# Two narrow first-stage units two turns later, and one copy of two chains on ScalarE

## The chip, the cores and the metric

The kernel runs on one core of a Trainium2 chip. The metric is the device time of one execution in microseconds (us). The engines are PE (TensorE, matmuls; PEld is its weight load), DVE (VectorE), ACT (ScalarE), POOL (GpSimd) and SP (SyncE, which here only issues DMA transfers). Each engine runs its own queue in order and waits on semaphores for the others.

## The reference

The input `x` is 8 batches of 2496 tokens with 256 channels. It is filtered in the frequency domain, and a soft mixture of experts with 8 experts of 4 slots follows over all 19968 tokens:

```
X = rfft(x, axis=1);  y = irfft(X * (filt_r + 1j*filt_i))
t = y.reshape(19968, 256)
logits = t @ phi                          # 32 slots
d = softmax over tokens (axis 0) of logits
slot_out[e] = relu((d.T @ t)[e] @ w1[e]) @ w2[e]
out = (softmax over slots (axis 1) of logits) @ slot_out
```

## The kernel before

The transform of 2496 = 39 x 64 points is done in two stages of matmuls. **First stage** (batches 1 to 7): each batch is cut into 6 pieces, `PIECE`, the piece 0 half as wide as the others. A piece is loaded to SBUF as `xt` (`load_x`, six buffers), folded into sums and differences `eo` (`fold_x`, L329, two elementwise instructions, on POOL but for the first pieces; two buffers), multiplied on PE (`s1_unit`, L346, matmuls at L357) into a PSUM tile of the pool `ps_s1`, which has one buffer (L264), copied by ACT to SBUF as `at` (L366, four buffers), and stored to `a_dram` in memory (`store_a`, L371). A piece of a batch is called unit (batch, piece) below. Batch 0 has a first stage of its own ahead of the loop.

**Main loop.** It runs over 80 turns n, ten a batch (`CPB = 10`), and writes out each turn's work in this order: loads of `ash` (the first stage's result, back from `a_dram`; `load_to`, L818), the load of one more `xt` and the fold of the units of turn n+1 (`split_next`, L788), the stores of the unit of the turn before, `t_unit` of turn n-2 (transposes, L467, ACT copies the result to `y`), `x_unit` of turn n (second-stage matmuls, L435; then DVE multiplies with the filter, `t2` at L455 and L457, and combines to `yt` at L458 and L459), the first-stage units of turn n, in odd turns `l_unit` (the logits, L494), and two steps of the chains (`hop_slot`, L861). At which turn a unit stands says `slot_of` (L78): the `ash` loads of a batch follow three turns behind its piece 5. In turns 33 to 37 stand (4,4), (5,0), (4,5), none, (5,1).

**Chains.** For each group of batches, (0,1), (2,3), (4,5), (6), (7), a generator `chain(g)` (L530) turns logits into running softmax weights and sums up the weighted tokens. Its steps run between the turns: transposes of the logits (`ltr`), inverse transforms (`v1`, `v`, `lg`), the maximum, the exponentials of `d` (DVE subtracts at L634, ACT exponentiates at L635, three pieces), their transform `u` (matmuls L528, ACT copies at L663), transposes of `u` (L525) copied to `u2` (L674), the transform `dd` (ACT copies at L682), the sums `z` and `s`. The first three chains take turns between two PSUM banks (`ps_c`, L263). In chains 0 to 2 the copy to `u2` goes in three parts, t0 = 0, 4 and 8, of 4, 4 and 2 transposes.

After the loop come the experts (weights loaded while the last turns run) and the output stage, whose stores end the execution.

Within the order of the program, the instructions of each engine are put in line when the kernel is built, by a planner that simulates them; `not_before` and `behind` add orders by hand, and the matmuls of `s1_unit` have high priority.

Of the kernel before, what the change touches and what calls it, by code (L numbers as in the profile page):

```python
# [39 lines left out]
NG = len(GROUPS)  # L40
# [8 lines left out]
CPB = NT // 2  # L49
# [4 lines left out]
NU = len(PIECE)  # L54
# [23 lines left out]
def slot_of(b, u):  # L78

    if b == 1:  # L80
        return u - 1
    if (b, u) in ((2, NU - 1), (3, 0)):
        return 2 * CPB - 6 + b - 2
    return CPB * b - 5 - (2 * (NU - 1 - u) if u else CPB + (b > 2))


def freq_of(t, c):
# [167 lines left out]
def fft_soft_moe(ctx, tc, x0, w0, x, ff, phi, wx, cst, w1q, sgn, out):  # L255
    nc = tc.nc
    pe, dve, act, pool_e, sp = nc.tensor, nc.vector, nc.scalar, nc.gpsimd, nc.sync
# [266 lines left out]
    def pe_t(*a):  # L524
        line(pe.transpose(*a))  # L525
# [4 lines left out]
    def chain(g):  # L530
# [6 lines left out]
        def psum(shape, name):  # L537
            pool, tag = banks[turn[0] % len(banks)]
            turn[0] += 1
            return pool.tile(shape, F32, tag=tag, name=name)  # L540
# [20 lines left out]
        for t0 in range(0, NT, 7):  # L561
# [3 lines left out]
            n = min(7, NT - t0)  # L565
# [19 lines left out]
        for s0 in range(0, NH, SA):  # L585
            n = min(SA, NH - s0)
# [6 lines left out]
        for s0 in range(0, NH, SA):  # L593
            n = min(SA, NH - s0)
# [33 lines left out]
        u = wk.tile([P, HT, 2 * N2], F32, tag="ca", name=f"u_{g}", bufs=1)  # L628
# [13 lines left out]
        for a0 in range(0, NH, 4):  # L642
            n = min(4, NH - a0)
            if a0 + 4 < NH and not late:
                dispatch(a0 + 4)
            pu = psum([P, 2, 4 * PK * 2, HT], f"u_{g}_{a0}")
# [19 lines left out]
        ended = [None, None]  # L666
        u2 = wk.tile([P, HT, 2, nb, SLOTS], F32, tag="cc", name=f"u2_{g}", bufs=1)
        dd = wk.tile([P, HT, 2, nb, SLOTS], F32, tag="cb", name=f"dd_{g}", bufs=1)
        for t0 in range(0, HT, TG):
            n = min(TG, HT - t0)  # L670
            pu = psum([P, TG, R], f"u2_{g}_{t0}")
            for t in range(n):
                pe_t(pu[:, t, :], u[0:R, t0 + t, :], ident[0:R, 0:R])
            ended[1] = dve.tensor_copy(u2[:, t0 : t0 + n].rearrange("k t h b e -> k t (h b e)"), pu[:, 0:n])  # L674
            yield f"u2_{t0}"
        for t0 in range(0, HT, TG):
            n = min(TG, HT - t0)
# [30 lines left out]
        for k, (ti, th, b2) in enumerate(terms):  # L708
            j = k % 4
            t = th * HT + ti  # L710
# [68 lines left out]
    for b, u in units[1:]:  # L779
        at_slot.setdefault(slot_of(b, u), []).append((b, u))  # L780
# [37 lines left out]
    def load_to(n):  # L818
        while loads:
            b, c = loads[0]  # L820
            if n < max(b * CPB + c - (3 if b < 2 else ASH), slot_of(b, NU - 1) + (2 if b < 3 else 3)):
                break
            load_ash(*loads.pop(0))
# [74 lines left out]
    for n in range(NS + LT):  # L898
        if n < NS:
            if n == slot_of(2, NU - 1) + 1:  # L900
                store_a()
            load_to(n)
            if n == CPB // 2:
                issue(cst_t[:, NEAR:FAR], cst[:, NEAR:FAR])
            if n == NS - 2 * CPB:
                behind("sp", sp.dma_start(cst_t[:, FAR:], cst[:, FAR:]))
            split_next(n + 1)
            store_a()
# [23 lines left out]
        if n >= LT:  # L932
            b, c = divmod(n - LT, CPB)
            if c % 2 == 1:
                l_unit(b, c)
            if c == CPB - 1 and b in last and b < BATCH - 1:
                active.append((last[b], chain(last[b])))
            if (b, c) == (BATCH - 1, CPB - 2):
                final = chain(NG - 1)
                for _ in range(3):  # L940
                    next(final)
# [11 lines left out]
    k = NS % YB - CPB  # L953
# [201 lines left out]
```

## Time and profile before

| | us |
|---|---|
| median of 3 runs (375.1 to 376.7) | 375.63 |
| profiled execution | 375.31 |
| its span, first to last instruction | 373.5 |
| PE busy in it | 344.2 |
| DVE, ACT, POOL busy in it | 264.6, 175.2, 147.0 |

The profiled execution takes 1.8 us more than its span. PE is the busiest engine; its granted clock is at the upper of its two levels (2.4 GHz) up to some 340 us, where the outputs are being stored, and at the lower one (1.2 GHz) behind that. How to read it: PE's time without work inside the loop is what one looks for, and what ends it. A wait for several semaphores is put down to the one that came last by the profile, so the engine named is not always the one that held things up.

### The profile page before, as it was taken

What the parts mean: (1) busy time and instruction counts of PE and PEld (TensorE: products, weight loads), DVE (VectorE), ACT (ScalarE), POOL (GpSimd) and SP (SyncE); (2) the same over time, 40 slices, a digit from 0 to 9 for tenths busy, and PEclk for the clock granted to TensorE, in tenths of its full rate; (3) what the DMA queues carried; (4) which work ended last, traced back from release to release, by engine and by line L of the source; (5) the groups of instructions that cost most, each with busy time, mean ns of one, the idle gap of its engine ahead of it and who ended that gap; (6) DMA issues with size and microseconds to landing.
All of it is one profiled execution on the core that took longest, in us unless ns stands there. A gap on an engine that the chain in (4) does not pass through costs nothing. (4 is left out here: it accounts for less than half of the span.)

```text
span 373.5 us, 10516 instructions
## 1 busy us (share of the span) xinstructions
PE 344.2 (92%) x4254; PEld 255.9 (69%) x4254; DVE 264.6 (71%) x522; ACT 175.2 (47%) x354; POOL 147.0 (39%) x177
## 2 busy tenths in 40 slices
PE   8999999899998899999889998899989999999950
PEld 6866766677776577867666775777866635878850
DVE  1586897778998969689996847695675552887540
ACT  3466554454555444545625453533354430766430
POOL 0188655545546213724830754332631302650000
PEclk9999999999999999999999999999999999999555
DMA  8999899799799459979853747642898993699996
GB/s 300 395 396 371 291 329 355 233 342 374 222 350 335 143 163 301 314 235 292 307 185 80 224 138 215 255 142 58 299 355 280 326 272 83 253 411 413 417 419 287
DMA packets 50438, 104.17 MB, mean 279 GB/s; under 512 B 5250, under 2 KB 23810, under 8 KB 48214
## 3 DMA queue, kind: packets, MB, share of 16 engines
q1 hardware_dynamic: 49700, 103.16, 79.4%
q8 instruction: 33, 0.54, 0.6%
q10 hardware_dynamic: 690, 0.35, 0.3%
q14 instruction: 15, 0.12, 0.1%
HBM read 63.37 MB, written 40.12 MB: 277 GB/s over the span
## 5 line engine op out<-in xcount | busy, mean ns | idle before, releaser
L435 PE MATMUL x<-cst_t,ash 128*128 128x128 f32 x640 | 85.7, 276 | 1.7 <-DMA ash<-a_dram 1.7
L455 DVE TENSOR_TENSOR t<-x,ff_t 128x512 f32<-128x512 f32 x80 | 55.1, 689 | 39.0 <-PE x L435 30.5
L336 POOL TENSOR_TENSOR eo<-xt 128x512 f32<-128x512 f32 (+1 forms) x37 | 45.2, 1220 | 94.4 <-issue 89.8
L435 PEld LDWEIGHTS x<-cst_t,ash 128*128 128x128 f32 x640 | 78.1, 192 | 4.0 <-DMA ash<-a_dram 2.6
L366 ACT COPY at<-s 128x1024 f32<-128x1024 f32 (+1 forms) x42 | 39.6, 942 | 47.8 <-PE s L357 27.8
L467 PE MATMUL t<-cst_t,yt 128*128 128x128 f32 x320 | 49.9, 278 | 0.0
L339 POOL TENSOR_TENSOR eo<-xt 128x512 f32<-128x512 f32 (+1 forms) x40 | 48.9, 1221 | 0.0
L481 ACT COPY y<-t 128x512 f32<-128x512 f32 x58 | 33.8, 587 | 30.8 <-PE t L467 30.5
L357 PE MATMUL s<-eo,w1q_t 64*64 64x512 f32 (+1 forms) x336 | 42.8, 579 | 2.7 <-POOL eo L339 2.5
L467 PEld LDWEIGHTS t<-cst_t,yt 128*128 128x128 f32 x320 | 35.9, 141 | 10.2 <-issue 7.1
L457 DVE TENSOR_TENSOR x<-x,ff_t 128x512 f32<-128x512 f32 x60 | 41.7, 696 | 1.3
L1104 PE MATMUL out<-so,st 32*128 32x256 f32 x468 | 35.1, 337 | 2.4 <-ACT ob L1109 1.3
L1104 PEld LDWEIGHTS out<-so,st 32*128 32x128 f32 x468 | 30.7, 222 | 6.1 <-ACT ob L1109 2.9
L494 PEld LDWEIGHTS l<-yt,phi_t 128*32 128x32 f32 x640 | 15.2, 109 | 25.5 <-issue 21.1
L1109 DVE COPY ob<-out 128x512 f32<-128x512 f32 (+1 forms) x40 | 25.0, 669 | 8.5 <-DMA out<-ob 5.8
L458 POOL TENSOR_TENSOR yt<-yt,t 128x256 f32<-128x256 f32 x20 | 15.1, 754 | 35.0 <-DVE yt L457 25.4
L1109 ACT COPY ob<-out 128x512 f32<-128x512 f32 (+1 forms) x40 | 21.7, 582 | 14.8 <-DMA out<-ob 7.8
L458 DVE TENSOR_TENSOR yt<-x,t 128x256 f32<-128x256 f32 x60 | 25.2, 420 | 1.3
L494 PE MATMUL l<-yt,phi_t 128*32 128x128 f32 x640 | 25.7, 278 | 0.0
L459 DVE TENSOR_TENSOR yt<-x,t 128x256 f32<-128x256 f32 x60 | 24.8, 413 | 0.0
L528 PE MATMUL s<-y,dd 128*32 128x256 f32 x232 | 19.2, 381 | 0.3 <-ACT dd L682 0.3
L528 PE MATMUL u<-cst_t,d 117*64 117x60 f32 (+3 forms) x440 | 15.2, 221 | 1.2 <-ACT d L635 1.2
(117 smaller groups left out, 482.1 us busy)
## 6 DMA issues: line engine op xcount, KB each, us to landing
xt<-in_x SPq DMA_DIRECT2D x35, 512.0 KB
ash<-a_dram SPq DMA_DIRECT2D x70, 256.0 KB
out<-ob SPq DMA_DIRECT2D x17, 1024.0 KB
a_dram<-at SPq DMA_DIRECT2D x56, 240.0 KB
w<-in_wx SPq DMA_DIRECT2D x33, 256.0 KB
w<-in_wx SPq DMA_DIRECT2D x6, 512.0 KB
x_t<-in_x SPq DMA_DIRECT2D x5, 512.0 KB
ff_t<-in_ff SPq DMA_DIRECT2D x10, 256.0 KB
```

Of the source, the lines that this page charges most:

```text
L336: ins = (dve if (1, 2) < (b, u) < (2, 0) else eng).tensor_tensor(out=eo[:, 0, 0:n], in0=xs[:, :, 0], in1=xs[:, :, 1], op=ALU.add)
L339: ins = eng.tensor_tensor(out=eo[:, 1, 0:n], in0=xs[:, :, 0], in1=xs[:, :, 1], op=ALU.subtract)
L357: ins = pe.matmul(ps, w1q_t[q, c], eo[q, c, 0:n], start=True, stop=True)
L366: act.copy(at[:, 0:n], both[:, :, 0:n].rearrange("q r u d -> q u r d"))
L435: ins = pe.matmul(ps[:, 2 * k + dh].rearrange("q r c -> q (r c)"), ash[:, k, dh * P : (dh + 1) * P], C("a1" if t0 + k else "b0"), start=Tr ...
L455: dve.tensor_tensor(out=t2, in0=ps[:, :, ::-1, :], in1=fiv, op=ALU.mult)
L457: dve.tensor_tensor(out=part, in0=ps, in1=frv, op=ALU.mult)
L458: add.tensor_tensor(out=yt[:, :, 1, :], in0=part[:, :, 1, :], in1=t2[:, :, 1, :], op=ALU.add)
L467: ins = pe.transpose(pt[:, k, dh, :], yt[:, c % 2, 2 * k + dh].rearrange("q r c -> q (r c)"), ident)
L494: ins = pe.matmul(pl[32 * j : 32 * j + 32, :], phi_t[:, dh, :], yt[:, j // 2, 2 * (j % 2) + dh].rearrange("q r c -> q (r c)"), start=(dh = ...
L1104: nc.tensor.matmul(prs[k][:, mm, :], sts[n][q, hs, c0 : c0 + P], so[q, ho], start=(i == 0), stop=(i == 2))
L1109: copy(ob[:, nm * k : nm * (k + 1), :], prs[k])
```

## The change

Two edits. In `slot_of`, the narrow unit of piece 0 stands at turn 10b - 16 for batches over 2 (one turn ahead of piece 5 of the batch before); for batches 5 and 7 it now stands at 10b - 14. So (5,0) goes from turn 34 to 36 and (7,0) from 54 to 56, and the order is (4,5), (5,0), (5,1) where it was (5,0), (4,5), (5,1). Its fold, its load's place in SP's queue and its stores go with it. In `chain`, the first of the three copies to `u2` (t0 = 0) is an ACT copy in the chains 0 and 1 (g < NG - 3 = 2) where it was a DVE copy.

```diff
--- before.py
+++ after.py
@@ -81,7 +81,7 @@
         return u - 1
     if (b, u) in ((2, NU - 1), (3, 0)):
         return 2 * CPB - 6 + b - 2
-    return CPB * b - 5 - (2 * (NU - 1 - u) if u else CPB + (b > 2))
+    return CPB * b - 5 - (2 * (NU - 1 - u) if u else CPB + (1, -1)[b in (5, 7)] * (b > 2))
 
 
 def freq_of(t, c):
@@ -671,7 +671,8 @@
             pu = psum([P, TG, R], f"u2_{g}_{t0}")
             for t in range(n):
                 pe_t(pu[:, t, :], u[0:R, t0 + t, :], ident[0:R, 0:R])
-            ended[1] = dve.tensor_copy(u2[:, t0 : t0 + n].rearrange("k t h b e -> k t (h b e)"), pu[:, 0:n])
+            copy = act.copy if t0 == 0 and g < NG - 3 else dve.tensor_copy
+            ended[1] = copy(u2[:, t0 : t0 + n].rearrange("k t h b e -> k t (h b e)"), pu[:, 0:n])
             yield f"u2_{t0}"
         for t0 in range(0, HT, TG):
             n = min(TG, HT - t0)
```

## Rows read from the trace of the kernel before

**Rows 1.** The page's first part: busy us, share, instructions of each engine.

```profile
PE 344.2 (92%) x4254; PEld 255.9 (69%) x4254; DVE 264.6 (71%) x522; ACT 175.2 (47%) x354; POOL 147.0 (39%) x177
```

**Rows 2.** Busy us of each engine (instructions) by stretches; then clock, DMA.

```profile
70.00:80.00 10.00, 10.00 (x110) 7.16 (x108) 9.47 (x20) 4.71 (x9) 3.94 (x4) 1.00 0.93 287
110.00:120.00 10.00, 8.75 (x136) 6.91 (x133) 8.63 (x15) 6.41 (x14) 8.03 (x6) 1.00 0.99 357
```

**Rows 3.** Waits of PE: engine, line, releaser: us in total, times, longest.

```profile
PE s L357 <- POOL eo L339: 2.5, 2, 1.2
PE u L525 <- DVE u L674: 1.7, 2, 0.9
PE x L435 <- DMA ash<-a_dram: 1.7, 4, 1.1
```

**Rows 4.** PE in order of time: start, us, line, out<-in, count, [idle before].

```profile
87.12 1.09 PE L357 MATMUL s<-eo,w1q_t 64*64 64x512 f32 x8
...
111.80 0.66 PE L357 MATMUL s<-eo,w1q_t 64*64 64x256 f32 x8
...
116.03 1.09 PE L357 MATMUL s<-eo,w1q_t 64*64 64x512 f32 x8 [1.25 <-POOL eo L339]
...
118.94 0.66 PE L467 MATMUL t<-cst_t,yt 128*128 128x128 f32 x4
```

**Rows 5.** The same of POOL: the folds of the first stage's inputs.

```profile
86.26 1.27 POOL L339 TENSOR_TENSOR eo<-xt 128x512 f32<-128x512 f32 x1
...
105.19 0.73 POOL L336 TENSOR_TENSOR eo<-xt 128x256 f32<-128x256 f32 x1 [2.58 <-issue]
...
110.88 1.28 POOL L339 TENSOR_TENSOR eo<-xt 128x512 f32<-128x512 f32 x1
112.63 1.82 POOL L336 TENSOR_TENSOR eo<-xt 128x512 f32<-128x512 f32 x1 [0.47 <-POOL eo L339]
114.40 1.59 POOL L339 TENSOR_TENSOR eo<-xt 128x512 f32<-128x512 f32 x1
```

**Rows 6.** The same of ACT, around the first wait.

```profile
114.89 0.52 ACT L635 ACTIVATE d<-d 117x384 f32<-117x384 f32 x1 [0.93 <-DVE d L634]
115.32 0.57 ACT L366 COPY at<-s 128x512 f32<-128x512 f32 x1
```

**Rows 7.** DVE's L634 from 111 us (ns min/median/max); then DVE in order.

```profile
L634 DVE TENSOR_TENSOR d<-lg,m_run x3: 679/1254/1631, 111.4 to 113.2; 117x512 f32<-117x512 f32 x2, 117x384 f32<-117x384 f32 x1
...
113.23 1.63 DVE L634 TENSOR_TENSOR d<-lg,m_run 117x384 f32<-117x384 f32 x1
...
117.03 0.41 DVE L459 TENSOR_TENSOR yt<-x,t 128x256 f32<-128x256 f32 x1
```

**Rows 8.** Order of time at the second place, DVE and PE.

```profile
182.65 1.25 DVE L694 TENSOR_TENSOR al<-m_run,m_run 128x32 f32<-128x32 f32 x1
...
183.90 1.09 PE L357 MATMUL s<-eo,w1q_t 64*64 64x512 f32 x8 [1.24 <-POOL eo L339]
...
186.17 0.41 DVE L459 TENSOR_TENSOR yt<-x,t 128x256 f32<-128x256 f32 x1
...
186.80 0.66 PE L467 MATMUL t<-cst_t,yt 128*128 128x128 f32 x4
```

**Rows 9.** The `u2` step of chain 0 in order; last, ACT copies grouped.

```profile
124.05 1.01 ACT L366 COPY at<-s 128x1024 f32<-128x1024 f32 x1 [2.07 <-issue]
...
125.09 1.28 DVE L674 COPY u<-u 128x512 f32<-128x512 f32 x2
...
125.83 0.44 PE L525 MATMUL u<-cst_t,u 128*128 128x128 f32 x2 [0.86 <-DVE u L674]
126.42 2.72 PE L528 MATMUL dd<-u,cst_t 128*128 128x512 f32 x8 [0.16 <-DVE u L674]
...
L481 ACT COPY y<-t 128x512 f32<-128x512 f32 x58 | 33.8, 587 | 30.8 <-PE t L467 30.5
```

**Rows 10.** Waits of SP's queue behind 255 us (columns as in rows 3).

```profile
SPq L882 <- PE ltr L525: 5.9, 1, 5.9
```

## The prediction

> **What bounds the kernel now.** I read the engines' totals first, then busy time by stretches of 10 us, then the waits of PE, and then the order of events around the longest of them. PE is busy 344.2 of 373.5 us [rows 1]; in an ordinary stretch of the main loop it is busy 10.00 of 10.00, and it falls to 8.75 in that from 110 to 120 us [rows 2]; the same pattern comes back 68 us later. So the loop is bound by PE, and what can be won there is PE's idle time. The waits of PE name two things that the change touches: two waits of a first-stage matmul (L357), 1.2 us each, and two of chain transposes (L525) on a DVE copy of `u2`, 0.9 us each [rows 3]. In these stretches PE has no other work that could fill them, since it runs its queue in order; each us of them should reach the end.
>
> **The first wait, and what ends it.** The narrow matmul at 111.80 is unit (5,0) (batch 5, piece 0, turn 34); the wide one at 116.03, with 1.25 us of idle PE before it, is (4,5) of turn 35 [rows 4]. The trace names the fold L339 that ends at 114.40 + 1.59 = 115.99 as the releaser. Counting folds against units, that is not this unit's fold: the narrow fold at 105.19 is that of (5,0), the next wide one, ending at 110.88 + 1.28 = 112.16, is that of (4,5), and the one from 112.63 is (5,1)'s, which could only start when (5,0) had freed one of the two `eo` buffers [rows 5]. Ten turns earlier the unit after a narrow one starts at 87.12 [rows 4] while the fold after it runs until 86.26 + 1.27 = 87.53 [rows 5]: such a unit doesn't need that fold. What it does need is the one PSUM tile of the first stage (`bufs=1`), freed by ScalarE's copy of (5,0). That copy runs from 115.32 to 115.89 although its matmuls ended at 112.46, because it is queued on ACT behind the exponentials of chain 0, the last at 114.89 [rows 4, 6]. So I take ACT's copy as the releaser: 115.89, then PE at 116.03.
>
> The exponentials are late because DVE's three subtractions (L634) are: 1.25, 0.68 and 1.63 us, the last one the smallest (384 columns) and the longest [rows 7]. Beside the first and the third a fold is on POOL, and the folds are stretched too, from 1.28 to 1.82 and 1.59 [rows 5]. The second (512 columns), 0.68, ran while that fold stood still; at its rate all three would take about 0.68 + 0.68 + 0.51 = 1.9, with overlap at their ends some 1.75 instead of 3.41 us. The Trainium skill (SBUF — State Buffer, section Who interferes with whom) says that a DVE instruction with two SBUF inputs and a GpSimd instruction that reads SBUF shut each other out for the whole instruction; the rows agree. By this rule the subtractions shrink once no fold lies beside them and the sum below stands, without it the backlog rival below (374.6) does.
>
> **Part 1: unit (5,0) to turn 36, (7,0) to turn 56.** Nothing is added or removed. What moves with a narrow unit: its eight matmuls on PE (0.66 us), two folds of 0.73 on POOL, one ACT copy of 0.57, two stores, and one load of `xt` issued a turn later.
> - PE: without the narrow unit the transposes of turn 35 start at 111.80, and (4,5) near 114.1 with a PSUM tile that was emptied before 111.80 and an `eo` ready long ago (its fold now follows (4,4)'s directly, so it starts near 105.2 instead of 109.6). The wait of 1.25 is gone; the 0.66 come back in turn 36. Gain 1.25.
> - What is late next? The transposes `t` of turn 36 need DVE's `yt` of turn 34, which ends at 117.03 + 0.41 = 117.44 now [rows 7]; they started at 118.94 [rows 4] and would start at about 118.94 - 1.25 - 0.66 = 117.0. But POOL: the narrow fold of (5,0) would run at 109.65 to 111.1, before the first subtraction at 111.45, and (5,1)'s starts only after (4,5), near 115.4. The subtractions then run alone, DVE is some 1.65 us earlier, `yt` is done near 115.8, and no wait appears.
> - The PSUM tile in turns 36 and 37: (4,5) ends near 115.2, its ACT copy of 1.0 near 117.0 at the latest; (5,0) comes at 118.6, its copy ends near 120, and (5,1) comes at 121.6. Each margin is about 1.6 us. The fold of (5,1) (2.5 us from 115.4) has 3.7 us of room.
> - SP: it is no longer held by (5,0)'s stores ahead of (4,5)'s. The two stores of (5,0) now stand ahead of the `ash` loads of batch 4, which turn 38 issues; the stores wait for a copy that ends near 120, so the loads stay where they are or come earlier. The `xt` load moved by a turn is wanted six units later.
>
> The second place repeats it: 1.24 us before the unit at 183.90; there DVE has one more operation behind POOL, `al`, 1.25 us for 32 columns [rows 8], where 256 columns of `yt` took 0.41. Together **1.25 + 1.24 = 2.5 us**.
>
> **Part 2: first `u2` copy on ScalarE, chains 0 and 1.** One 128x512 copy of each chain moves: on DVE two took 1.28 together, on ACT the like copy takes 0.587 [rows 9]. The chain has two PSUM banks, so the third pair of transposes waits for the first copy. Now both copies queue on DVE from 125.09, behind a turn's elementwise work, and the third transposes start at 125.83, the `dd` matmuls at 126.42 [rows 9]. After: ACT takes the first copy, but it is itself in the wide copy of (5,1), 124.05 to 125.06 [rows 9], so it can start near 124.97 and end at 125.56; the transposes go at about 125.64 (0.19 earlier). DVE copies the second bank from 125.09 to about 125.75, where it was second in line and ended at 126.37; so `dd` no longer waits 0.16. Gain 0.19 + 0.16 = 0.35 a chain. The bounds: 0.86 + 0.16 = 1.02 if ACT were free in time; and 0.19 - 1.01 = -0.8 if a further wide ACT copy slips ahead. I take 0.35, since the wide copy stands ahead by data. ACT is busy 47% of the span [rows 1] and sat idle 2.07 us ahead of that wide copy, so 0.59 more on it is hidden by idle time; without that it would push back the next copy by as much. Two chains: **0.7 us**.
>
> **Does it reach the end?** Towards the end of the loop the weight loads (L882) hang on PE: SP waited 5.9 us for a transposition, L525, before one of them [rows 10]; so they start earlier with PE. The outputs at the end follow the last stage. So I pass the whole on: 375.31 - 2.5 - 0.7 = 372.1 for the profiled execution, which is 0.3 under the median of 375.63; beside that median, **372.4 us**.
>
> **Rivals**, on the median's scale:
> - *Only the move counts*, `u2` brings nothing as the copy ends no earlier on ACT: 375.6 - 2.5 = 373.1. For it: the wide copy ahead on ACT. Chance 0.12. The other way, ACT free in time: 375.6 - 2.5 - 2.0 = 371.1, chance 0.04.
> - *DVE's backlog takes the wait's place.* If the subtractions stay at 3.4 us without the folds, turn 36 waits for `yt` until 117.5 (gain 118.94 - 117.5 - 0.66 = 0.8), and at the second place `yt` ends at 186.17 + 0.41 = 186.58 against a start at 186.80 [rows 8], so 0.2 - 0.66 = -0.45. Together 0.35, with part 2: 374.6. For it: DVE's two places are close behind PE. Against: the second subtraction's 0.68. Chance 0.11.
> - *The change doesn't do what it says*: the unit in turn 35 waits for POOL, as the trace names it, or the same bank wait shows up once in turn 36 or 37; part 2 alone is left: 374.9. Chance 0.11.
> - *Slower: two bank waits for one.* Three first-stage units now stand in turns 35, 36 and 37 and share one PSUM tile. If ACT's order puts chain 0's `u` copies ahead of the copies of (4,5) and (5,0), both next units wait as the one does now: 1.25 more at each place, less 0.35, so 2 x 0.9 = 1.8: 377.4. It decides when such a copy slips by over 1.6 us. Chance 0.08.
>
> **How the numbers follow.** The forecast has 0.54, with a range of its own of 371.6 to 373.0. To hold 8 in 10 I go from 370.9 (the better `u2`) to 375.0 (past both cases near 374.7). A measurement here can tell about 0.5% from no change, 1.9 us, so faster means under 373.75: 0.54 + 0.12 + 0.04 = 0.70; same 0.22; slower 0.08.
>
> **What would show it.** Right: no idle PE before the wide L357 near 114 and 182 us; three L634 in under 2 us; one `u2` copy on ACT right behind a wide `at` copy; the third transposes about 0.2 us less late. Wrong: a wait of 1 us on L357 elsewhere in turns 35 to 37, transposes `t` waiting for DVE, an `ash` wait of over the 1.1 us seen before [rows 3], or a stretch behind 200 us that grows by what the loop gave.

## The result, and the profile after

The changed kernel takes **370.83 us** (370.04 to 371.53, 5 runs) where the kernel before took 375.52 beside it (375.1 to 376.7, 5 runs): ratio 0.987, 95% interval 0.985 to 0.989, so 4.7 us less. Run once more it took 370.91 against 375.36, ratio 0.988 (0.986 to 0.990). The forecast was 372.4 with a range from 370.9: the direction is as forecast, the gain is half as large again as the 3.2 us of the sum, and the time lies 0.07 us below the range.

The page's first part for the changed kernel, to be held against [rows 1], and then busy time by stretches, against [rows 2]:

```profile
PE 344.4 (93%) x4254; PEld 257.9 (70%) x4254; DVE 259.0 (70%) x520; ACT 177.4 (48%) x356; POOL 144.7 (39%) x177
```

```profile
70.00:80.00 10.00, 10.00 (x109) 7.74 (x108) 9.43 (x20) 5.23 (x9) 3.93 (x4) 1.00 0.96 304
110.00:120.00 10.00, 10.00 (x169) 8.01 (x166) 7.72 (x18) 6.34 (x14) 3.93 (x4) 1.00 1.03 380
```

PE does the same work, 344.4 us of it, and the stretch from 110 to 120 us, where it had been busy 8.75, is now as full as an ordinary one. DVE is busy 5.6 us less although only 1.3 us of copies left it: the rest is operations that had been stretched.

The waits of PE (engine, line, releaser: us in total, times, longest), against [rows 3]:

```profile
PE x L435 <- DMA ash<-a_dram: 4.0, 3, 1.8
...
PE t L467 <- DVE yt L459: 0.3, 1, 0.3
...
PE s L357 <- ACT at L366: 0.2, 1, 0.2
```

Both waits that the change touches are gone from the list: L357 behind POOL, and L525 behind the DVE copy to `u2`. (The 0.2 us of L357 behind `at` lie at 22 us and stand in the kernel before as well.) One wait of 0.3 us of `t` for `yt` is new. The waits for `ash` are longer than in [rows 3]; they lie at 46, 53 and 69 us, ahead of all that the change moves, and the table below takes them up.

The first place, in order of time (start, us, engine, line, out<-in, count, [idle before]):

```profile
114.06 1.09 PE L357 MATMUL s<-eo,w1q_t 64*64 64x512 f32 x8
...
120.29 0.66 PE L357 MATMUL s<-eo,w1q_t 64*64 64x256 f32 x8
...
122.27 1.04 PE L525 MATMUL u<-cst_t,u 128*128 128x128 f32 x8
123.24 1.09 PE L357 MATMUL s<-eo,w1q_t 64*64 64x512 f32 x8
124.26 0.44 PE L525 MATMUL u<-cst_t,u 128*128 128x128 f32 x2
124.59 2.72 PE L528 MATMUL dd<-u,cst_t 128*128 128x512 f32 x8
...
112.38 1.76 DVE L634 TENSOR_TENSOR d<-lg,m_run 117x512 f32<-117x512 f32 x3
...
122.91 0.59 ACT L675 COPY u<-u 128x512 f32<-128x512 f32 x1 [1.26 <-PE u L525]
124.44 1.01 ACT L366 COPY at<-s 128x1024 f32<-128x1024 f32 x1 [0.94 <-PE s L357]
```

Three things are to be seen. The wide unit (4,5) at 114.06 starts without a wait, as do (5,0) at 120.29 and (5,1) at 123.24. The three subtractions of L634 take 1.76 us where they took 3.41 ([rows 7]: 0.68 to 1.63 each). And PE's **order** around `u2` is another: in the kernel before, the wide unit (5,1) stood ahead of the eight transposes; here the transposes come first, at 122.27, and the unit of 1.0 us stands between them and the last two transposes. The copies to `u2` run under that unit, and nobody waits for them. At the second place the subtractions take 1.76 us as well. There the first operation on `al`, 1.25 us in [rows 8], takes 0.18; the second one (L697), 0.18 in the kernel before, now lies beside a fold and takes 0.69. One wait of `t` is left:

```profile
179.40 0.18 DVE L695 TENSOR_TENSOR al<-m_run,m_run 128x32 f32<-128x32 f32 x1
...
181.30 0.69 DVE L697 TENSOR_TENSOR al<-al,cst_t 128x32 f32<-128x32 f32 x1
...
183.40 0.63 PE L467 MATMUL t<-cst_t,yt 128*128 128x128 f32 x4 [0.32 <-DVE yt L459]
```

To see where 4.7 us come from, I took the starts of a few matmuls from each kernel's timeline of PE: (4,4) in turn 33 and (6,4) in turn 53, the first `z` of chains 0, 1 and 2, the first `h` of the experts, and the first `out`. Differences in us, of one profiled execution each:

| kernel | to (4,4) | (4,4) to z0 | z0 to (6,4) | (6,4) to z1 | z1 to z2 | z2 to h | h to out | out to the end |
|---|---|---|---|---|---|---|---|---|
| before | 108.39 | 20.91 | 46.96 | 20.91 | 56.79 | 45.74 | 18.71 | 55.1 |
| after | 109.32 | 18.15 | 47.19 | 18.52 | 57.02 | 45.73 | 18.72 | 55.1 |
| move alone | 107.88 | 18.62 | 46.95 | 18.99 | 56.78 | 45.73 | 18.72 | 55.1 |
| ACT copy alone | 108.62 | 20.32 | 47.19 | 20.32 | 57.02 | 45.73 | 18.72 | 55.1 |
| after, unit first | 108.52 | 18.95 | 47.19 | 19.31 | 57.02 | 45.73 | 18.72 | 55.1 |
| copy and order, no move | 108.38 | 19.51 | 47.19 | 19.51 | 57.11 | 45.74 | 18.71 | 55.1 |
| fold held | 107.80 | 19.88 | 46.95 | 19.89 | 56.78 | 45.75 | 18.71 | 55.0 |
| copy ahead | 109.21 | 21.21 | 47.32 | 24.00 | 56.77 | 45.76 | 18.71 | 55.1 |
| two pins | 109.31 | 18.15 | 46.95 | 18.16 | 56.79 | 45.74 | 18.71 | 55.1 |
| three pins | 107.69 | 18.15 | 46.96 | 18.15 | 56.58 | 45.74 | 18.72 | 55.1 |
| both held | 108.20 | 18.15 | 46.95 | 18.15 | 56.33 | 45.73 | 18.72 | 55.1 |
| after, again | 109.93 | 18.16 | 47.19 | 18.50 | 57.04 | 45.74 | 18.72 | 55.0 |

A column that an edit doesn't reach comes back within some 0.05 us (z2 to h: 45.73 to 45.76), so differences of 0.1 us can be read. From before to after: -2.76 + 0.23 - 2.39 + 0.23 - 0.01 + 0.01 = **-4.69**, which is the difference of the medians. So close an agreement is in part luck: in the kernels of the experiments the sum of these columns and the difference of the medians lie up to 0.8 us apart (copy and order: 2.25 against 3.02), and 1.3 us for copy ahead. The columns are the finer measure. What stands ahead of (4,4) varies from 107.7 to 109.9 among the twelve executions, with no relation to the edits to be seen (after, after again and the three kernels with pins run the same up to there and span the whole range); there lie the waits for `ash` (4.0 us in total in this execution of after, 1.7 in that of before). They are left out of what follows.

### The profile page after: what moved, and what is told of

Its sections match the earlier page's. It is cut to its first block, busy times and chain, and to the rows that moved or that the text cites. A ratio compares the mean times of both kernels' runs of the same rounds, so it can differ in the third digit from the quotient of the medians.

```text
span 369.7 us, 10512 instructions
## 1 busy us (share of the span) xinstructions
PE 344.4 (93%) x4254; PEld 257.9 (70%) x4254; DVE 259.0 (70%) x520; ACT 177.4 (48%) x356; POOL 144.7 (39%) x177
## 4 chain that ended last, share of the span: by engine, by line
PE 80%; DVE 7%; DMA 4%; ACT 4%; issue 2%; SPq 0%; DVEq 0%; ACTq 0%
PE x L435 17%; PE s L357 9%; PE t L467 9%; PE out L1105 7%; PE s L528 5%; PE l L494 5%; PE u L528 3%; PE v L528 3%; DMA ash<-a_dram 3%; PE s L408 3%; PE lg L528 3%; PE dd L528 3%; PE h L1049 2%; PE o L1067 2%; PE v L525 2%
## 5 line engine op out<-in xcount | busy, mean ns | idle before, releaser
L336 POOL TENSOR_TENSOR eo<-xt 128x512 f32<-128x512 f32 (+1 forms) x37 | 44.0, 1189 | 92.9 <-issue 86.9
L339 POOL TENSOR_TENSOR eo<-xt 128x512 f32<-128x512 f32 (+1 forms) x40 | 48.3, 1208 | 0.0
L357 PE MATMUL s<-eo,w1q_t 64*64 64x512 f32 (+1 forms) x336 | 42.8, 579 | 0.2 <-ACT at L366 0.2
L1105 PE MATMUL out<-so,st 32*128 32x256 f32 x468 | 36.1, 368 | 1.1 <-DVE ob L1110 0.8
L1105 PEld LDWEIGHTS out<-so,st 32*128 32x128 f32 x468 | 32.8, 254 | 3.7 <-DVE ob L1110 1.7
L494 PE MATMUL l<-yt,phi_t 128*32 128x128 f32 x640 | 26.5, 279 | 0.0
L481 ACT COPY yb<-t 128x512 f32<-128x512 f32 x20 | 11.7, 586 | 11.6 <-PE t L467 11.6
```

The costliest lines, as they stand in the source:

```text
L336: ins = (dve if (1, 2) < (b, u) < (2, 0) else eng).tensor_tensor(out=eo[:, 0, 0:n], in0=xs[:, :, 0], in1=xs[:, :, 1], op=ALU.add)
L339: ins = eng.tensor_tensor(out=eo[:, 1, 0:n], in0=xs[:, :, 0], in1=xs[:, :, 1], op=ALU.subtract)
L357: ins = pe.matmul(ps, w1q_t[q, c], eo[q, c, 0:n], start=True, stop=True)
L481: act.copy(y, pt.rearrange("k p h d -> k p (h d)"))
L494: ins = pe.matmul(pl[32 * j : 32 * j + 32, :], phi_t[:, dh, :], yt[:, j // 2, 2 * (j % 2) + dh].rearrange("q r c -> q (r c)"), start=(dh = ...
L1105: nc.tensor.matmul(prs[k][:, mm, :], sts[n][q, hs, c0 : c0 + P], so[q, ho], start=(i == 0), stop=(i == 2))
```

## The experiments

Three theories were to be told apart; the expectations call them A, B and C. A: the gain over the forecast comes from PE's new order around `u2`, where the unit covers the copies. B: the move leaves the `u2` step as it was, as the forecast had it. C: the copy on ScalarE gives nothing, and all is in the move. The names of the headings are those of the table. The kernel before took 376.12 us beside the first four experiments and 375.56 beside fold held, copy ahead, two pins and three pins. In the diffs, statements that share a line are shown one below the other, and some lines that only set up or fill a table are left out.

### Move alone

```diff
-    return CPB * b - 5 - (2 * (NU - 1 - u) if u else CPB + (b > 2))
+    return CPB * b - 5 - (2 * (NU - 1 - u) if u else CPB + (1, -1)[b in (5, 7)] * (b > 2))
```

> Part 1 alone (the two narrow units two turns later, all copies to u2 on DVE). The planner's order of PE is that of the changed kernel: the eight transposes of u stand ahead of the wide unit (5,1). Theory A (each part gives its own waits, and the extra over my forecast comes from the transposes standing ahead of that unit): the bank wait is gone, 1.2 us a place; of the u2 step's 1.25 us about 0.75 are won, because the unit now covers the first DVE copy but dd still waits some 0.5 us for the second one, which stands behind L457 on DVE: 375.5 - 2.4 - 1.5 = 371.6. Theory B (my blind working: the u2 step is untouched by the move): 375.5 - 2.5 = 373.0. Theory C (the copy on ScalarE gives nothing, all is in the move): 370.8.

Measured: 371.29 against 376.12, ratio 0.988 (0.986 to 0.990). The move by itself brings nearly all: 2.29 and 1.92 us at the two places. By the table that is 4.2 us, between theory A's 3.9 and theory C's 4.7, and by the medians 4.8; the next three kernels decide between them. Its order of time, PE and then DVE:

```profile
120.83 1.04 PE L525 MATMUL u<-cst_t,u 128*128 128x128 f32 x8
121.80 1.09 PE L357 MATMUL s<-eo,w1q_t 64*64 64x512 f32 x8
122.82 0.44 PE L525 MATMUL u<-cst_t,u 128*128 128x128 f32 x2
123.62 2.72 PE L528 MATMUL dd<-u,cst_t 128*128 128x512 f32 x8 [0.36 <-DVE u L674]
...
121.69 0.68 DVE L674 COPY u<-u 128x512 f32<-128x512 f32 x1
...
122.88 0.68 DVE L674 COPY u<-u 128x512 f32<-128x512 f32 x1
```

The transposes stand ahead of the wide unit here too: the planner changed PE's order because of the move, not because of ScalarE's copy. With it both copies on DVE are nearly in time; the last two transposes don't wait, and `dd` waits 0.36.

### ACT copy alone

```diff
+            copy = act.copy if t0 == 0 and g < NG - 3 else dve.tensor_copy
-            ended[1] = dve.tensor_copy(u2[:, t0 : t0 + n].rearrange("k t h b e -> k t (h b e)"), pu[:, 0:n])
+            ended[1] = copy(u2[:, t0 : t0 + n].rearrange("k t h b e -> k t (h b e)"), pu[:, 0:n])
```

> Part 2 alone (first copy to u2 on ScalarE in chains 0 and 1, units where they were). On PE the wide unit still stands ahead of the transposes, on ACT its wide copy ahead of the copy to u2. Theories A and B: the bank wait of 1.25 us stays, the u2 step wins 0.35 us a chain: 374.8. Theory C: nothing, 375.5.

Measured: 374.97, ratio 0.997 (0.996 to 0.999). PE and ACT at the step that [rows 9] shows of before:

```profile
123.08 1.09 PE L357 MATMUL s<-eo,w1q_t 64*64 64x512 f32 x8
124.10 1.09 PE L525 MATMUL u<-cst_t,u 128*128 128x128 f32 x8
125.84 0.44 PE L525 MATMUL u<-cst_t,u 128*128 128x128 f32 x2 [0.64 <-ACT u L675]
126.11 2.15 PE L528 MATMUL dd<-u,cst_t 128*128 128x512 f32 x6
...
124.28 1.01 ACT L366 COPY at<-s 128x1024 f32<-128x1024 f32 x1 [2.08 <-issue]
125.19 0.59 ACT L675 COPY u<-u 128x512 f32<-128x512 f32 x1
```

Here the unit is ahead of the transposes, as in the kernel before, and the copy queues on ACT behind the wide copy of that unit: this is the picture of the forecast. The wait before the last transposes falls from 0.86 to 0.64 and that of `dd` goes. The stage shortens by 0.59, and 0.23 of it is lost again in the stretch behind `z` (two pins, below): 0.36 a chain, where 0.35 was forecast. That the copy alone gains refutes theory C.

### After, unit first

The changed kernel with the first transpose held behind the unit (`held[1]` is the unit's last matmul), so that PE has the order of the kernel before.

```diff
+        _ = not_before(u2_first[b // 2 - 2], held[1]) if (b, u) in ((5, 1), (7, 1)) else None
...
-                pe_t(pu[:, t, :], u[0:R, t0 + t, :], ident[0:R, 0:R])
+                ins = pe.transpose(pu[:, t, :], u[0:R, t0 + t, :], ident[0:R, 0:R])
+                line(ins)
+                u2_first.setdefault(g, ins)
```

> The changed kernel with the transposes of u put behind the wide unit of their turn on PE, as they stood before; nothing else is asked for, and ACT's wide copy then stands ahead of the copy to u2 again. Theory A: the u2 step loses 0.9 us a chain against the changed kernel: 372.4 to 372.6, which is my blind forecast. Theory C: no difference, 370.8.

Measured: 372.45, ratio 0.990 (0.988 to 0.992).

```profile
121.56 1.09 PE L357 MATMUL s<-eo,w1q_t 64*64 64x512 f32 x8
122.58 1.09 PE L673 MATMUL u<-cst_t,u 128*128 128x128 f32 x8
124.32 0.44 PE L673 MATMUL u<-cst_t,u 128*128 128x128 f32 x2 [0.64 <-ACT u L675]
...
122.77 1.01 ACT L366 COPY at<-s 128x1024 f32<-128x1024 f32 x1 [1.92 <-PE s L357]
123.67 0.59 ACT L675 COPY u<-u 128x512 f32<-128x512 f32 x1
```

Both edits of the change are in, the unit has its old place, and the wait of 0.64 us is back. This is the kernel that the forecast had in mind: by the table it takes 1.96 - 0.23 + 1.60 - 0.23 = 3.1 us less than the kernel before, where 3.2 was forecast (the medians differ by 3.7). The order alone is worth 0.80 and 0.79 us at the two places.

### Copy and order, no move

The kernel before with ScalarE's copy, and with the matmuls of the units (5,1) and (7,1) held behind the last of the eight transposes (`u2_last`).

```diff
+                _ = not_before(ins, u2_last[b // 2 - 2, 4]) if (b, u) in ((5, 1), (7, 1)) else None
...
+            copy = act.copy if t0 == 0 and g < NG - 3 else dve.tensor_copy
```

> The kernel before with the first copy to u2 on ScalarE and the transposes of u put ahead of the wide unit (5,1) and (7,1); the narrow units stay in turns 34 and 54. Theory A: the bank wait of 1.25 us stays, the u2 step wins all of its 1.25 us a chain: 375.5 - 2.5 = 373.0. Theory B: 0.35 a chain, 374.8. Theory C: 375.5.

Measured: 373.1, ratio 0.992 (0.990 to 0.994). Against the copy alone the order brings 20.32 - 19.51 = 0.81 at each place, the same as with the move; the wait of 1.25 before (4,5) stays. The time is theory A's (373.0); B had 374.8 and C 375.5. So with ScalarE's copy in, the effects of the move and of the order add up and don't depend on each other. What the order is worth with both copies on DVE was not measured by itself.

### Fold held

The kernel before, with the fold of (5,1) (and (7,1)), `first_ins`, on POOL waiting for the third subtraction. Every engine's order is unchanged.

```diff
+        if (b, u) in ((5, 1), (7, 1)):
+            info = mybir.DependencyInfo(mybir.DependencyClass.Sync, mybir.DependencyReason.DATA)
+            tc.add_manual_dep(first_ins.ins, subs[b // 2 - 2].ins.name, info, reason="after the subtractions")
...
+            subs[g] = dve.tensor_tensor(out=d[:, x0:x1], in0=lgf[:, x0:x1], in1=mb, op=ALU.subtract)
```

> The kernel before with one added wait: the fold of (5,1) and of (7,1) on POOL starts only when the chain's third subtraction on DVE is done. The order of every engine is that of before. Theory lock (fold and subtraction shut each other out, and late subtractions make the exponentials and with them ACT's copy of the narrow unit late): the second and third subtraction take 0.6 and 0.5 us, the copy is done near 114.6, the wide unit doesn't wait; 1.2 us at each place: 376.1 - 2.4 = 373.7. Rival (the subtractions are slow of themselves, 1.25 to 1.63 us): no gain there, and the later fold makes it worse: 376.1 or above.

Measured: 373.49, ratio 0.995 (0.993 to 0.997). The subtractions (ns min/median/max), then PE, POOL and ACT:

```profile
L634 DVE TENSOR_TENSOR d<-lg,m_run x3: 545/677/1253, 110.9 to 112.6; 117x512 f32<-117x512 f32 x2, 117x384 f32<-117x384 f32 x1
```

```profile
114.41 1.09 PE L357 MATMUL s<-eo,w1q_t 64*64 64x512 f32 x8 [0.21 <-ACT at L366]
...
113.42 1.28 POOL L336 TENSOR_TENSOR eo<-xt 128x512 f32<-128x512 f32 x1 [1.85 <-PE x L435]
114.65 1.28 POOL L339 TENSOR_TENSOR eo<-xt 128x512 f32<-128x512 f32 x1
...
113.70 0.57 ACT L366 COPY at<-s 128x512 f32<-128x512 f32 x1
```

This settles two disputed steps. First the releaser: the unit at 114.41 starts while the fold that the trace had named (L339, here until 114.65 + 1.28 = 115.93) still runs; it starts right behind ScalarE's copy of the narrow unit, 113.70 + 0.57 = 114.27, and that is now the releaser named. Then the lock: without the fold beside it the third subtraction takes 545 ns where it took 1631, and both halves of the fold take 1.28 where they took 1.82 and 1.59 [rows 5]; the first subtraction, beside the tail of the earlier fold, still takes 1253. The Trainium skill (SBUF — State Buffer, section Who interferes with whom) has a DVE instruction with two SBUF inputs and a GpSimd instruction that reads SBUF shut each other out; each of these four numbers agrees. The gain is 1.03 and 1.02 us at the two places, where 1.2 was expected: holding one fold back brings about half of what the move does there (2.29 and 1.92).

### Copy ahead

The kernel before, with ScalarE's copy of the narrow unit put ahead of the third exponential: the bank is free early, and the lock stays.

```diff
+        ins = act.copy(at[:, 0:n], both[:, :, 0:n].rearrange("q r u d -> q u r d"))
+        _ = not_before(third[b // 2 - 2], ins) if (b, u) in ((5, 0), (7, 0)) else None
...
+            third[g] = act.activation(d[:, x0:x1], d[:, x0:x1], AF.Exp)
```

> The kernel before with ACT's copy of the narrow unit, (5,0) and (7,0), put ahead of the third exponential of the chain on ACT's queue; the fold of (5,1) on POOL stays beside the subtractions. What ends the wait of the wide unit at 116.03? Theory bank (the one PSUM tile, freed by ACT's copy): that copy ends near 114.6, the wait of 1.25 us before the wide unit is gone though the fold L339 still ends near 116.0. At the first place the 1.2 us are kept; at the second the transposes of turn 56 then wait for DVE's yt, whose 186.58 lies only 0.2 us ahead of 186.80, so about 0.2 is kept: 376.1 - 1.4 = 374.7. Theory fold (the releaser that the trace names): the wide unit still waits until the fold ends, 1.25 us at each place: 376.1.

Measured: 378.02 against 375.56, ratio 1.006 (1.004 to 1.009): **slower**. PE at the first place, with POOL and ACT beside it, then PE and DVE at the second:

```profile
115.41 1.09 PE L357 MATMUL s<-eo,w1q_t 64*64 64x512 f32 x8
...
126.02 0.44 PE L525 MATMUL u<-cst_t,u 128*128 128x128 f32 x2 [1.40 <-DVE u L674]
126.61 3.88 PE L528 MATMUL dd<-u,cst_t 128*128 128x512 f32 x8 [0.16 <-DVE u L674]
...
115.22 1.60 POOL L339 TENSOR_TENSOR eo<-xt 128x512 f32<-128x512 f32 x1
...
114.69 0.57 ACT L366 COPY at<-s 128x512 f32<-128x512 f32 x1
...
189.26 1.05 PE L467 MATMUL t<-cst_t,yt 128*128 128x128 f32 x4 [2.12 <-DVE alc L698]
...
186.62 1.23 DVE L696 TENSOR_TENSOR al<-al,cst_t 128x32 f32<-128x32 f32 x1
```

The bank wait is gone here too, with the fold running until 116.82: the copy is what PE had waited for. But neither of the two times that were expected came out. The subtractions still take 3.41 us, and DVE gains less than PE: counted from (4,4), the copies to `u2` start 0.6 us earlier than in the kernel before, the first eight transposes 1.2 us, so the waits before the last transposes grow from 0.86 to 1.40 us each. At the second place the second operation on `al` takes 1.23 us beside a fold, and `t` waits 2.12 us. (It waits for `yt`, which ends at 189.11; `t` doesn't read the `alc` that the trace names.) This is the backlog rival, come true at the second place of a kernel that keeps the lock. After the second of these, and after the 1.40 at the first place, the granted clock falls (columns as in [rows 2]):

```profile
188.00:189.00 1.00, 0.00 (x0) 0.00 (x0) 1.00 (x3) 0.24 (x1) 0.00 (x0) 1.00 0.93 251
...
190.00:191.00 1.00, 1.00 (x7) 1.00 (x6) 0.60 (x2) 0.00 (x0) 0.00 (x0) 0.50 0.00 0
```

The lower clock makes up most of the loss in this execution. At the first place the stretch from `dd` to `z` takes 3.81 us where it took 2.88 before; at the second the matmuls from this `t` to the next take 4.07 us where the same ones took 2.53 at the first. That is 0.93 + 1.54 = 2.5 of the 3.4 us that the two places lose together (table: 0.30 + 3.09). By this estimate the first place would have won 0.6 us without it, and the second still lost 1.5.

### Two pins, three pins, both held

These ask what is left in the changed kernel, by orders alone. Two pins: DVE finishes `yt` of turn 34 (54) ahead of the products of turn 35 (55), and the logits `l` of turn 37 (57) stand behind a whole group of four `s` matmuls. Three pins: besides, one of POOL's two additions of turn 68's `yt` waits for the third subtraction of chain 2. Both held: so does the other. In the diff the first two blocks are the two pins (a DVE product behind the last addition of the turn before; the first logit matmul behind `s` term 31), and the last two lines the third and the fourth.

```diff
+        if (b, c) in ((3, 5), (5, 5)):
+            not_before(ins, add_of[b, c - 1])
...
+                        if (b, c) in ((3, 5), (5, 5)):
+                            not_before(ins, s_term[b // 2 - 1, 31])
...
+            if g == 2 and a0 == 8:
+                tc.add_manual_dep(add_first[6, 8].ins, ins.ins.name, info, reason="after the subtractions")
+                tc.add_manual_dep(add_of[6, 8].ins, ins.ins.name, info, reason="after the subtractions")
```

> The changed kernel with two orders pinned that its planner had turned: DVE finishes turn 34's (54's) yt before it starts turn 35's (55's) products, and the logits of turn 37 (57) stand behind a whole group of four s matmuls on PE and not inside one. Theory A: the wait of 0.3 us of the transposes in turn 56 goes, and the stretches behind z, which are 0.23 us longer each than in the kernel before, go back to their length: 0.75 us under the changed kernel, ratio to before 0.985. Rival: the 0.23 us are not from the group that is broken up, 0.3 us only, ratio 0.986.

> As e7_two_pins, and in chain 2 POOL's two additions of turn 68's yt start only when the chain's third subtraction is done. Theory lock: the three subtractions take 1.8 us where they took 2.85, the first exponential starts 0.6 us earlier, and the wait of 1.2 us of the u matmuls for it falls to about 0.6; ratio to before 0.983. Rival: the transposes of turn 70 then wait for the additions and give it back: as e7_two_pins.

> Differs from the run with three pins only in that both of POOL's two additions of turn 68's yt wait for chain 2's third subtraction, where only the first of the two was held and the second ran beside the first subtraction (2.32 us each instead of the 1.8 of the undisturbed threes). If the shared lock of POOL and DVE is what stretches them, the three subtractions come down to about 1.8 us, and the span from the first z matmul of chain 1 to that of chain 2 shortens by the part of 0.5 us that the u matmuls' wait shows there: ratio about 0.983 of the kernel before. If the additions are then late for yt and t of chain 2 instead, the wait moves to t and nothing is gained: 0.985.

> The changed kernel once more, on the same chip as the run beside it and with as many rounds: 0.987 if the first comparison was typical. Between its first matmul of unit (4,4) and the first z matmul of chain 0 it should again show about 18.2 us, and between (6,4) and z of chain 1 about 18.5; what differs from the first profile should be in the early waits for ash alone.

Measured: two pins 370.66, ratio 0.986 (0.984 to 0.988); three pins 369.85, 0.985 (0.982 to 0.987); both held 369.71 against 375.36, 0.986 (0.983 to 0.988), beside the changed kernel on the same chip at 370.91. Against that neighbour the table has 0.01 + 0.24 + 0.35 + 0.71 = 1.31 us less, the medians 1.2. The three versions can't be told apart by their whole times, but their stages can.

The 0.23 us behind `z` first, in the changed kernel and then with two pins:

```profile
131.25 0.51 PE L494 MATMUL l<-yt,phi_t 128*32 128x128 f32 x11
131.52 0.38 PE L528 MATMUL s<-yb,dd 128*32 128x256 f32 x1
131.58 0.28 PE L494 MATMUL l<-yt,phi_t 128*32 128x128 f32 x3
```

```profile
131.24 0.62 PE L498 MATMUL l<-yt,phi_t 128*32 128x128 f32 x16
131.68 0.38 PE L718 MATMUL s<-y,dd 128*32 128x256 f32 x1
...
131.70 0.38 PE L718 MATMUL s<-yb,dd 128*32 128x256 f32 x1
```

The `s` matmuls go in fours that run side by side, each on 32 columns. In the changed kernel the logits start inside such a group (three of it at 131.04 and 131.05), and its last matmul, on `yb`, runs at 131.52 among them; the other kernels with ScalarE's copy show the same 47.19 in the column z0 to (6,4). Behind a whole group the column is at 46.95 again, as in the kernel before. The pin on DVE takes the 0.32 us wait of `t` at the second place ((6,4) to z1: 18.52 to 18.16). Chain 2, in the changed kernel and with both additions held:

```profile
232.15 2.38 DVE L634 TENSOR_TENSOR d<-lg,m_run 117x512 f32<-117x512 f32 x2
...
234.11 2.28 PE L528 MATMUL u<-cst_t,d 117*64 117x60 f32 x64 [1.18 <-ACT d L635]
```

```profile
230.19 1.76 DVE L641 TENSOR_TENSOR d<-lg,m_run 117x512 f32<-117x512 f32 x3
...
231.89 2.08 PE L535 MATMUL u<-cst_t,d 117*64 117x60 f32 x64 [0.91 <-ACT d L646]
```

Three pins missed what was expected of it: with one addition still beside them the three subtractions took 2.32 us, not 1.8, and the wait of the `u` matmuls stayed at 1.18. With both additions held all three take 1.76 with nothing of POOL beside them, where they took 2.85 in the changed kernel (the first two 2.38), and z1 to z2 falls by 0.25 beyond what the one addition gave (56.58 to 56.33). The wait of the `u` matmuls is shorter by 0.27 than in the changed kernel; 0.91 of it stays, behind the first exponential. The lock is thus shown at a third place, between DVE's subtractions and POOL's additions of `yt`; the ratio of 0.983 that was expected lies at the edge of the interval, as 0.25 us is less than the whole times can tell.

## Why the prediction was right, and where it was wrong

| step of the prediction | forecast us | measured us | read from |
|---|---|---|---|
| the wait before the wide unit, two places | 2.5 | 2.4 | ACT copy alone to unit first: 1.37 + 1.01 |
| ScalarE's copy, two chains | 0.7 | 0.7 | before to ACT copy alone: 2 x (0.59 - 0.23) |
| PE's order around `u2` | not in the sum | 1.6 | unit first to after: 0.80 + 0.79 |
| sum | 3.2 | 4.7 | |

The split holds for the edits taken in this order. Put in behind the move, which brings the new order along, ScalarE's copy is worth 0.47 us a place less the 0.23 lost behind `z`, 0.5 us in all.

- **What bounds the kernel.** Right: each us of PE's idle time in these stretches reached the end. The columns behind z2 are the same in both kernels, and the columns' sum is the difference of the medians.
- **The releaser.** Right, against the name in the trace: ScalarE's copy of the one PSUM tile, shown by two kernels in which the unit starts while the fold still runs.
- **The lock.** Right: three subtractions alone in 1.76 us, some 1.75 forecast; the first operation on `al` at the second place takes 0.18 in the changed kernel where [rows 8] has 1.25. The kernel with the copy ahead shows that part 1 needs this beside the free bank: with the bank free and the lock kept the kernel is slower. By the estimate above most of that loss is the lower clock behind the longer waits; without it the two places together would still lose 0.9 us.
- **Nothing late next.** Right at the first place. At the second `t` waits 0.32 us for `yt`: a small piece of the backlog rival, since DVE took the products of both turns, and the 0.69 us of `al` beside a fold, ahead of the first turn's `yt`. The pin on DVE's order removes it. It is why the second place gives 1.01 and not 1.37.
- **Part 2, ScalarE's copy.** The 0.35 a chain came out for the order that it assumed (0.36), but by luck, as the net of two errors: the copy brings 0.59, as the step to `dd` shortens by more than the idle time that the trace puts there, and 0.23 is lost in the `s` groups.
- **The step that failed** is in part 2: "I take 0.35, since the wide copy stands ahead by data." That rests on the unit (5,1) standing ahead of the transposes on PE, which was read from the trace of before. No data sets it; the planner does, and moving a unit made it plan anew. The new order was worth 0.80 and 0.79 us, which the sum has at nothing. With the unit behind the transposes its 1.0 us covers the copies, ScalarE is free when the first is due ([1.26] idle ahead of it), and the wide copy follows. The rival "ACT free in time", 371.1, is near what happened, yet I gave it 0.04, because I judged ScalarE's queue and took PE's as fixed. The bound was in the text (1.02 us a chain), though it too was low: copy and order together bring 20.91 - 19.51 = 1.40 a chain, 1.2 net of the loss behind `z`. What was missing was the edit's effect on an order that a planner makes.
- **The other rivals.** Only the move counts: it had 2.5 us less, but the move alone brings 4.2 by the table (4.8 by the medians), again for the order. Two bank waits: none is seen. The change doing nothing: refuted by the waits.
- **The signs named ahead.** Two of the four for right came: no idle PE before the wide units, three L634 under 2 us. Two didn't: the copy on ACT stands ahead of a wide `at` copy, not behind one, and the last transposes don't wait at all. These two are the miss, visible in one view. Of the signs named as wrong, two came. The transposes `t` wait for DVE once, 0.32 us, at the second place. An `ash` wait over 1.1 us came (1.8), but at 53 us, ahead of anything that moved, and the median shows no loss from it.

What stays open: why the planner puts the transposes first once the narrow unit has moved (the traces show what it chose, not what it weighed), and why the waits for `ash` ahead of (4,4) vary by 2 us from one execution to another.

## What to carry to other kernels

When a planner or a scheduler lines up the instructions, an edit that moves one piece moves others: price the step next to it once with the order of the trace and once with the neighbours swapped, and give the second its own chance. A unit of independent matmuls is best placed where its time covers a copy that the next matmuls wait for; here that was worth 0.8 us a place. And where an engine is named as releaser, count instances and look at who else must finish. Freeing a resource early can lose time while the lateness behind it, here that of DVE's operations beside POOL's, stays.

## What the runs showed of the hardware beyond that

**The granted clock fell after waits within the loop.** In the kernel with the copy ahead, TensorE's granted clock went from 1.00 to 0.50, its lower level of 1.2 GHz, after PE had been idle for 2.12 us, and came back some 3.4 us later; at the first place the same followed a wait of 1.4 us before the last transposes. The matmuls behind were longer: the eight `dd` took 3.88 us where [rows 9] has 2.72, four `t` 1.05 where [rows 4] has 0.66. The length of the wait doesn't decide it alone: at the second place the same wait of 1.40 us ahead of the last transposes left the eight `dd` at 2.72. In the kernel before, the waits of 1.25 and 0.86 us in the same stretches left the clock at 1.00. So two of these waits cost more than their length. That profiled execution was 1.8 us above its kernel's median, so how often this happens isn't known.

**A group of four broken up.** Logit matmuls put behind three of a group of four `s` matmuls, and not behind the whole group, cost 0.23 us each time (47.19 against 46.95 in the column z0 to (6,4), 57.02 against 56.79 in z1 to z2).
